# Second reciprocal spread as three bf16 parts, its split on VectorE around the first scales, and selectors built while the first inputs land

## The chip, the cores and the metric

One core of one Trainium2 chip. The metric is the device time of one execution in microseconds (us); most kernels ran several times, and all those runs are of the fast state; three kernels ran only once, which leaves their state unknown, and of these only the profiles are used. A profile is one execution; its span is some 1.8 us shorter than the time that is reported for it (291.8 against 293.62 for the first one).

## The reference

Linear attention with the feature map elu(x) + 1 over 8 batches, 8 heads, 576 tokens and a head width of 64, then a two-layer network with g(h) = h - tanh(h).

```python
def phi(x): return np.where(x > 0, x, np.exp(x) - 1.0) + 1.0
q_p, k_p = (phi(q), phi(k))
kv = np.einsum('bhsd,bhse->bhde', k_p, v)
z = np.sum(k_p, axis=2)
num = np.einsum('bhsd,bhde->bhse', q_p, kv)
den = np.einsum('bhsd,bhd->bhs', q_p, z)[..., None] + 1e-06
# x = (num / den), heads side by side: [4608, 512]
h = x @ w_in                 # [4608, 2048]
out = (h - np.tanh(h)) @ w_out   # [4608, 512]
```

All inputs are fp32 in memory. The loads that GpSimd issues turn them into bf16 on the way.

## The kernel before

The token axis is worked in nine chunks of 512. TensorE writes into banks numbered 0 to 7, and another engine has to empty a bank before it is written again. Before chunk 0 can begin, batch 0 has to pass through attention; this opening fills the first 18 us or so. 1/den lies as one row per token group and head (`rden`), and it must be spread over the 64 channels of each head. TensorE does this with a matmul by a 0/1 selector, a "spread". In batch 0 the spread is fp32, for head pairs 0 and 2 first, for 1 and 3 later:

```python
    def b0_spread(pairs, n0):
        for n, p in enumerate(pairs):
            for t in range(4):
                r = slice(32 * t, 32 * t + 32)
                nc.tensor.matmul(ps_all[:, 4 + t, 128 * (n0 + n):128 * (n0 + n) + 128],
                                 sel[r, p].rearrange("p h e -> p (h e)"), rden_t[0][r, 0:128], start=True, stop=True)
    ...
    load_q(0)
    load_k(0)
    make_identity(nc, ident)      # GpSimd, as the loads
    load_v(0)
    ...                           # w_in in ten pieces
    load_k(1); load_wo(0); load_wo(1); load_q(1)
    ...                           # GpSimd memsets
    load_v(1); load_wo(2); load_wo(3)
    ...
    b0_spread((0, 2), 0)
    b0_scale(0, ns0, 0, 0, 4)
    b0_scale(0, ns0, 0, 4, 8)
    b0_scale(2, ns0, 1)
    b0_num(1, ns0)                # TensorE into banks 2 and 3, then a ScalarE copy out of them

    def open2():
        b0_spread((1, 3), 2)
        b0_scale(1, ns0, 2)
        b0_scale(3, ns0, 3)
    ...
    # chunk 0, hidden blocks 0 to 3 in banks 0 to 3, as (head pair, block)
            order = [((0, 0), (0, 1)), ((2, 0), (2, 1), (0, 2), (0, 3), (2, 2), (2, 3)),
                     [(p, fi) for p in (1, 3) for fi in range(4)]]
            for n, part_ in enumerate(order):
                if n == 1:
                    open2()
                ...
```

In the second layer of chunk 0 TensorE goes through four groups of four steps, one quarter of `w_out` for each group. Batch 1's attention lies between these steps: its q is transposed and its k and v are multiplied just ahead of the third group. In batch 1 the spread is already done from three bf16 parts that lie in three bands of the rows, so that one matmul adds them up (`a_split`, with the selector `sel3`); `prepare` builds that selector on VectorE in the second layer of chunk 0.

Of the kernel before, what the change touches and what calls it, by code (L numbers as in the profile page):

```python
# [18 lines left out]
def kernel(  # L19
# [80 lines left out]
    def load_q(b):  # L100
        q_t[b] = kpool.tile([128, 2, 2, J, D], BF16, name="qraw")
        load(b, q_t[b], q, b == 0)
# [124 lines left out]
    def b0_num(i, ns):  # L227
# [4 lines left out]
                             qT[:, i, 0:8, hg, :], start=True, stop=True)  # L232
        nc.scalar.copy(ns[:, i::2, 0:8, :].rearrange("p a j t -> p a (j t)"), ps_all[:, b0:b0 + 2, :])

    def b0_spread(pairs, n0):

        for n, p in enumerate(pairs):
# [4 lines that stand above are left out]
# [164 lines left out]
    act0 = rpool.tile([128, 1], F32, name="act0")  # L406
    nc.scalar.activation(act0, zero[:, 0:1], AF.Exp)
    load_q(0)
    load_k(0)
    make_identity(nc, ident)  # L410
    load_v(0)
    for f0, n in ((0, 256), (256, 256), (512, 512), (1024, 512), (1536, 512)):
        load_wi(f0, n)
# [22 lines left out]
    for n in range(3):  # L436
        e0 = float(np.float32(rest).astype(ml_dtypes.bfloat16))
        nc.vector.memset(eps[32 * n:32 * n + 1], e0)
        rest -= e0


    def spin(n):
        for _ in range(n):
# [2 lines left out]
    side = Banks([4, 5, 6, 7])  # L446
    kz_t[0] = kz_c[0]
    (eq0, rq0, mq0), (eq1, rq1, mq1) = (phi_pieces(0, q_t, qp_t, "qp", i) for i in range(2))
    for f in (eq0, rq0, mq0, eq1, rq1, mq1):
        f()  # L450
    spin(18)
# [3 lines left out]
        f()  # L455
    spin(5)
    a_qT_pe(0, 1, side, "AA")

    for t in range(4):
        nc.scalar.copy(s8[32 * t:32 * t + 32, 0].rearrange("q h p -> q (h p)"),  # L460
                       ident[32 * t:32 * t + 32, 32 * t:32 * t + 8])
    nc.scalar.copy(sel, s8[:, 0].rearrange("q h p -> q p h").unsqueeze(3).to_broadcast([128, NP, 2, 64]))
    spin(6)
    b0_z(0)
# [10 lines left out]
    b0_num(0, ns0)  # L475
    b0_kv(1)
    b0_kz(1)
    b0_spread((0, 2), 0)

    b0_scale(0, ns0, 0, 0, 4)  # L480
    b0_scale(0, ns0, 0, 4, 8)
    b0_scale(2, ns0, 1)
    b0_num(1, ns0)

    def open2():
        b0_spread((1, 3), 2)
        b0_scale(1, ns0, 2)
        b0_scale(3, ns0, 3)

    def prepare():  # L490

        for t in range(4):
            nc.vector.tensor_copy(s8[32 * t:32 * t + 32, 1:3].rearrange("q n h p -> q (n h p)"),
                                  ident[32 * t:32 * t + 32, 32 * t + 8:32 * t + 24])
        s24 = rpool.tile([128, 2 * NP], F32, name="s24")
        f8 = s8.rearrange("q n h p -> q n (h p)")
        nc.vector.tensor_add(s24, f8[:, 1], f8[:, 2])
        nc.vector.tensor_reduce(part[:, 0:1], s24, mybir.AxisListType.X, ALU.add, negate=True)
        nc.vector.tensor_reduce(part[:, 1:2], f8[:, 2], mybir.AxisListType.X, ALU.add, negate=True)
        nc.vector.tensor_add(s24, s24, f8[:, 0])  # L500
        nc.vector.tensor_copy(
            sel3, s24.rearrange("q (h p) -> q p h", h=2).unsqueeze(3).to_broadcast([128, NP, 2, 64]))

    for c in range(NC):
        gT = gpool.tile([128, NF, 512], BF16, name="gT")
        n1, n2 = c + 1, c + 2
        s1 = {i: [] for i in range(16)}
        s2 = {i: [] for i in range(16)}
        if c == 0:
            side = Banks([4, 5, 6, 7])  # L510
            sub = {}

            def spread1(h):
                sub["bp"] = a_spread_pe(1, 4, (2 * h, 2 * h + 1))
                for p in (2 * h, 2 * h + 1):
                    a_scale(1, p, sub["ns"], sub["bp"], 144 * (p % 2))

            def num1():
                sub["ns"] = new_ns(1)
                for p in (NP, 0, 1, 2, 3):  # L520
                    a_num_copy(1, sub["ns"], p, side)

            s1[11].append(lambda: a_kphi(1, 0))
            s1[13].append(lambda: a_kphi(1, 1))
            s2[3].append(lambda: a_qphi(1, 0))
            s2[4].append(lambda: (a_qphi(1, 1), load_q(2), load_k(2), load_v(2)))
            s2[0].append(prepare)
            s2[7].append(lambda: (a_qT_pe(1, 0, side), a_kv(1, side), a_qT_pe(1, 1, side)))
            s2[8].append(lambda: b0_scale_rest(side))
            s2[9].append(lambda: (a_den(1, side), num1(), a_split(1)))  # L530
            s2[11].append(lambda: spread1(0))

            qs, ks = [], []

            def exp2(pieces, src, store, name, i):
                pieces.append(phi_pieces(2, src, store, name, i))
                pieces[i][0]()

            def rest2(f):
                f[1]()  # L540
                f[2]()

            s2[11].append(lambda: (exp2(qs, q_t, qp_t, "qp", 0), rest2(qs[0])))
            s2[12].append(lambda: exp2(qs, q_t, qp_t, "qp", 1))
            s2[13].append(lambda: (spread1(1), exp2(ks, k_t, kp_t, "kp", 0), rest2(qs[1]), a_qT_dma(2)))
            s2[14].append(lambda: rest2(ks[0]))
        elif n1 < B:
            s1[8 if c == 1 else 5].append(lambda: a_kv_cols(n1, attn))
            s1[10 if c == 1 else 8].append(lambda: (a_den(n1, attn), a_spread(n1)))
            for p in range(NP + 1):  # L550
                s2[(11 if c == 1 else 9) + p].append(lambda p=p: a_num(n1, p))
        if c == 1:
            s1[1].append(lambda: a_kphi(2, 1))
            s1[3].append(lambda: (a_vp(2, 0), a_vp(2, 1)))
        if c >= 1 and n2 < B:

            s1[0].append(lambda: (gate(qT_t[n1]), load_k(n2), load_q(n2), load_v(n2)))
            d = 2
            s2[d].append(lambda: a_kphi(n2, 0))
            s2[d + 2].append(lambda: a_kphi(n2, 1))  # L560
            s2[d + 4].append(lambda: a_qphi(n2, 0))
            s2[d + 6].append(lambda: (a_qphi(n2, 1), a_qT_dma(n2)))
            for i in range(2):
                s2[14 + i].append(lambda i=i: a_vp(n2, i))
        if c == 0:

            first = Banks([4, 5, 6, 7, 0, 1, 2, 3])
            hs = [ps_all[:, n, :] for n in range(4)]
            order = [((0, 0), (0, 1)), ((2, 0), (2, 1), (0, 2), (0, 3), (2, 2), (2, 3)),
                     [(p, fi) for p in (1, 3) for fi in range(4)]]  # L570
            seen = [0] * 4
            for n, part_ in enumerate(order):
                if n == 1:
                    open2()
                for x in range(2 if n == 0 else 0):
                    for p, fi in part_:
                        nc.tensor.matmul(hs[fi][:, 256 * x:256 * x + 256], w_in_sb[:, 0, fi * 128:(fi + 1) * 128],
                                         xT[:, p, 256 * x:256 * x + 256], start=(x == 0), stop=False)
                        seen[fi] = 1
                for p, fi in part_ if n else ():  # L580
                    l1mm(c, fi, hs[fi], p, seen[fi])
                    seen[fi] += 1
            for fi in range(4):
                l1act(fi, hs[fi], gT)
        for fi in range(4 if c == 0 else 0, NF):
            h = first() if c == 0 else dense()
            for p in range(NP):
                l1mm(c, fi, h, p, p)
            if c == 0:
                l1act(fi, h, gT)  # L590
            elif fi % 2:
                n = dense.order[(dense.n - 1) % 6]
                l1act2(fi - 1, ps_all[:, n - 1:n + 1, :], gT)
            for f in s1[fi]:
                f()
        os_ = {}
        for s in range(16):

            (g, i) = divmod(s, 4) if c == 0 else (s % 4, s // 4)
            if g == 0:  # L600
                os_[i] = ps_all[:, i, :] if c == 0 else dense()
            if c == NC - 1 and i == 3:

                if g == 0:
                    o2 = dense()
                    for o, f in ((os_[i], slice(0, 384)), (o2, slice(384, DM))):
                        for fi in range(NF):
                            nc.tensor.matmul(o[:, f], gT[:, fi, 384:512], w_out_sb[:, fi, f],
                                             start=(fi == 0), stop=(fi == NF - 1))
                        evac(c, i, o, f.start, f.stop)  # L610
                continue
            l2mm(gT, os_[i], i, 4 * g, 4 * g + 4)
            if g == 3:
                evac(c, i, os_[i])
            for f in s2[s]:
                f()
# [30 lines left out]
```

## Time and profile before

| | before |
|---|---|
| time, median of the first 3 runs | 294.0 us (293.95 to 294.2) |
| span of the profile | 291.8 us |
| TensorE busy | 284.2 us, 97% |
| first spread starts | 14.79 us |
| second layer of chunk 0 starts | 31.10 us |
| third quarter of `w_out` lands | 40.89 us |

A page has one row for each engine over 40 equal slices. The views used here are the timeline (start, duration, engine, line, operation, output and inputs, count, and in brackets the idle time before it with what ended it), the chain that ended last (start, duration, what), and the table of windows (window, length, then the busy time of PE, PEld, DVE, ACT and POOL, granted clock, share of the transfer engines, GB/s). PE is TensorE, PEld its weight loads, DVE VectorE, ACT ScalarE, POOL GpSimd. Line numbers differ between kernels.

### The profile page before, as it was taken

What the parts mean: (1) busy time and instruction counts of PE and PEld (TensorE: products, weight loads), DVE (VectorE), ACT (ScalarE), POOL (GpSimd) and SP (SyncE); (2) the same over time, 40 slices, a digit from 0 to 9 for tenths busy, and PEclk for the clock granted to TensorE, in tenths of its full rate; (3) what the DMA queues carried; (4) which work ended last, traced back from release to release, by engine and by line L of the source; (5) the groups of instructions that cost most, each with busy time, mean ns of one, the idle gap of its engine ahead of it and who ended that gap; (6) DMA issues with size and microseconds to landing.
All of it is one profiled execution on the core that took longest, in us unless ns stands there. A gap on an engine that the chain in (4) does not pass through costs nothing.

```text
span 291.8 us, 4476 instructions
## 1 busy us (share of the span) xinstructions
PE 284.2 (97%) x1775; PEld 134.5 (46%) x1803; DVE 174.8 (60%) x266; ACT 139.7 (48%) x168; POOL 33.1 (11%) x55
## 2 busy tenths in 40 slices
PE   8999999999999999999999999999999999999994
PEld 3544464454454444544444445444444444444443
DVE  4759958987458674776478637865581457106600
ACT  4838638846254733465345534751551155126411
POOL 8673030110030003000300030000000000000000
PEclk9999999999999999999999999999999999999999
DMA  6999999998989668955795579766117310130032
GB/s 96 198 204 212 208 207 213 214 168 145 253 158 159 170 131 135 200 139 127 134 223 131 120 137 196 144 142 139 32 34 168 73 36 0 42 84 20 0 74 72
DMA packets 39077, 38.94 MB, mean 133 GB/s; under 512 B 16336, under 2 KB 33808, under 8 KB 38288
## 3 DMA queue, kind: packets, MB, share of 16 engines
q0 software_dynamic: 17552, 18.35, 39.0%
q1 hardware_dynamic: 21344, 20.17, 30.5%
q8 instruction: 14, 0.23, 0.3%
q10 hardware_dynamic: 160, 0.13, 0.1%
q14 instruction: 7, 0.06, 0.1%
HBM read 43.91 MB, written 9.55 MB: 183 GB/s over the span
## 4 chain that ended last, share of the span: by engine, by line
PE 75%; DMA 18%; POOL 2%; issue 1%; SPq 1%; DVE 1%; ACT 1%; DVEq 0%; POOLq 0%
PE ps_all L366 37%; PE ps_all L387 32%; DMA w_out_sb<-in_moe_w_out_dram 6%; DMA w_in_sb<-in_moe_w_in_dram 3%; DMA rdb<-ds 3%; DMA out_dram<-osb 2%; PE ps_all L199 2%; DMA kraw<-in_k_dram 2%; PE ps_all L317 2%; DMA ds<-rden 1%; PE ps_all L276 1%; POOL v L419 1%; ACT osb L396 1%; SPq L401 0%; POOL qraw L90 0%
## 5 line engine op out<-in xcount | busy, mean ns | idle before, releaser
L366 PE MATMUL ps_all<-xT,w_in_sb 128*128 128x512 bf16 x558 | 126.5, 380 | 0.9 <-issue 0.2
L387 PE MATMUL ps_all<-w_out_sb,gT 128*128 128x512 bf16 x548 | 126.2, 380 | 0.7
L373 DVE TENSOR_TENSOR gT<-ps_all,th 128x1024 bf16<-128x1024 f32 x64 | 77.9, 1218 | 59.7 <-ACT th L372 59.7
L372 ACT ACTIVATE th<-ps_all 128x1024 f32<-128x1024 f32 x64 | 65.5, 1023 | 57.0 <-PE ps_all L366 46.4
L366 PEld LDWEIGHTS <-w_in_sb 128*128 128x128 bf16 x574 | 55.0, 98 | 66.0
L387 PEld LDWEIGHTS <-gT 128*128 128x128 bf16 x560 | 54.1, 98 | 64.7 <-issue 0.6
L396 ACT COPY osb<-ps_all 128x512 f32<-128x512 f32 (+1 forms) x36 | 20.8, 582 | 72.3 <-PE ps_all L387 55.9
L328 DVE TENSOR_TENSOR xT<-ps_all,rdb 128x512 bf16<-128x512 f32 x24 | 16.3, 689 | 13.7 <-PE ps_all L317 11.2
L134 ACT ACTIVATE e<-qraw 128x1152 bf16<-128x1152 bf16 x16 | 18.5, 1161 | 7.3 <-DMA qraw<-in_q_dram 7.3
L134 ACT ACTIVATE e<-kraw 128x1152 bf16<-128x1152 bf16 x15 | 17.4, 1162 | 0.1
L136 DVE TENSOR_TENSOR qp<-e,r 128x1152 bf16<-128x1152 bf16 x16 | 12.1, 758 | 7.8 <-ACT e L134 7.0
L136 DVE TENSOR_TENSOR kp<-e,r 128x1152 bf16<-128x1152 bf16 x15 | 11.4, 758 | 7.9 <-ACT e L134 7.0
L383 POOL COPY g<-qT 1x1 bf16<-1x1 bf16 x5 | 0.9, 182 | 119.7 <-DMA qT<-qp 119.7
L378 DVE TENSOR_TENSOR gT<-ps_all,th 128x512 bf16<-128x512 f32 x16 | 10.3, 686 | 2.3 <-ACT th L377 1.7
L377 ACT ACTIVATE th<-ps_all 128x512 f32<-128x512 f32 x16 | 9.2, 598 | 4.4 <-PE ps_all L366 3.2
L444 PE MATMUL ps_all<-zero 128*128 128x512 bf16 x29 | 9.3, 487 | 1.2 <-DVE zero L405 1.2
L317 PE MATMUL ps_all<-qT,kz 128*128 128x512 bf16 x28 | 10.1, 380 | 0.1
L135 DVE TENSOR_SCALAR r<-qraw 128x1152 bf16<-128x1152 bf16 x16 | 7.3, 453 | 1.9 <-DMA qraw<-in_q_dram 1.9
L199 PEld LDWEIGHTS <-kp 64*128 64x128 bf16 x216 | 6.4, 94 | 2.5 <-issue 2.5
L285 DVE RECIPROCAL rden<-den 128x144 f32<-128x144 f32 x7 | 7.4, 1052 | 0.2
L199 PE MATMUL ps_all<-vp,kp 64*128 64x136 bf16 x216 | 7.4, 220 | 0.0
L394 DVE COPY osb<-ps_all 128x128 f32<-128x128 f32 x1 | 0.3, 291 | 11.6 <-DMA out_dram<-osb 11.6
(84 smaller groups left out, 123.0 us busy)
## 6 DMA issues: line engine op xcount, KB each, us to landing
out_dram<-osb SPq DMA_DIRECT2D x70, 128.0 KB
rdb<-ds SPq DMA_DIRECT2D x12, 576.0 KB
kraw<-in_k_dram POOLq DMA_DIRECT2D x7, 576.0 KB, 7.1
qraw<-in_q_dram POOLq DMA_DIRECT2D x7, 576.0 KB, 9.2
v<-in_v_dram POOLq DMA_DIRECT2D x7, 576.0 KB, 11.9
w_out_sb<-in_moe_w_out_dram POOLq DMA_DIRECT2D x4, 512.0 KB, 16.0
w_in_sb<-in_moe_w_in_dram POOLq DMA_DIRECT2D x6, 256.0 KB, 8.6
qraw<-in_q_dram POOLq DMA_DIRECT2D x2, 288.0 KB, 4.4
```

What stands on the lines that cost most here:

```text
L134: return (lambda: nc.scalar.activation(e, x, AF.Exp), lambda: nc.vector.tensor_scalar(r, x, 0.0, 1.0, ALU.max, ALU.add), lambda: nc.vector ...
L136: lambda: nc.vector.tensor_tensor(y, e, r, ALU.min))
L199: nc.tensor.matmul(ps[hg][:, i, :], kp[r, i, j].rearrange("p h d -> p (h d)"), vp[r, i, j, :], start=(j == 0), stop=(j == J - 1))
L317: nc.tensor.matmul(ps, kz[:, p // 2, p % 2, 0:128], qT[:, p % 2, 0:8, p // 2, :], start=True, stop=True)
L328: nc.vector.tensor_mul(xT[:, p, S * b:S * b + 512].rearrange("p (j t c) -> p j t c", j=8, t=4), ps.rearrange("p j (t c) -> p j t c", t=4), ...
L366: nc.tensor.matmul(h, w_in_sb[:, 2 * (p % 2) + p // 2, fi * 128:(fi + 1) * 128], xT[:, p, c * 512:(c + 1) * 512], start=(n == 0), stop=(n ...
L372: nc.scalar.activation(th, h, AF.Tanh)
L373: nc.vector.tensor_sub(gT[:, fi:fi + 2, :], h, th)
L378: nc.vector.tensor_sub(gT[:, fi, :], h, th)
L387: nc.tensor.matmul(o, gT[:, fi, i * 128:(i + 1) * 128], w_out_sb[:, fi, :], start=(fi == 0), stop=(fi == NF - 1))
L396: nc.scalar.copy(osb[:, f0:f1], o[:, f0:f1])
L444: nc.tensor.matmul(ps_all[:, 0, :], zero[:, 0:128], zero, start=True, stop=True)
```

## The change

The intent is to shorten TensorE's work in the opening. The second spread takes three bf16 parts instead of fp32. The parts are made on VectorE, the first half of the work ahead of the first scales, in a hole, and the second half behind them. Since their selector is now needed at the start, `prepare` moves there, and the identity that it reads goes ahead of k on GpSimd. On TensorE three dense matmuls go ahead of the second spread, to cover the wait for the parts.

```diff
+    def b0_split():
+        f = rden_t[0][:, 0:128]
+        t1, t2, w = (rpool.tile([128, J * 16], BF16, name=n)[:, 0:128] for n in ("t1", "t2", "w"))
+        u = rpool.tile([128, J * 16], F32, name="u")[:, 0:128]
+        nc.vector.tensor_copy(t1, f)
+        nc.vector.scalar_tensor_tensor(u, t1, part[:, 0:1], f, ALU.mult, ALU.add)
+        yield
+        nc.vector.tensor_copy(t2, u)
+        nc.vector.scalar_tensor_tensor(w, t2, part[:, 1:2], u, ALU.mult, ALU.add)
+        rden_t[0] = w
+        yield
+    def b0_spread3(pairs, n0):        # as b0_spread, with sel3 and w
 ...
     load_q(0)
+    make_identity(nc, ident)
     load_k(0)
-    make_identity(nc, ident)
 ...
+    prepare()                         # ahead of the first work on q; its code is moved here
-    for t in range(4):
-        nc.scalar.copy(s8[32 * t:32 * t + 32, 0]...,  ident[...])
 ...
+    split0 = b0_split()
+    next(split0)
     b0_spread((0, 2), 0)
     b0_scale(0, ns0, 0, 0, 4)
     b0_scale(0, ns0, 0, 4, 8)
     b0_scale(2, ns0, 1)
+    next(split0)
     b0_num(1, ns0)
     def open2():
-        b0_spread((1, 3), 2)
+        b0_spread3((1, 3), 2)
 ...
-            s2[0].append(prepare)
 ...
-            order = [((0, 0), (0, 1)), ((2, 0), (2, 1), (0, 2), (0, 3), (2, 2), (2, 3)),
+            order = [((0, 0), (0, 1)), ((0, 2), (0, 3), (2, 0)), ((2, 1), (2, 2), (2, 3)),
                      [(p, fi) for p in (1, 3) for fi in range(4)]]
-                if n == 1:
+                if n == 2:
                     open2()
```

More of the change, by code (lines that the diff above doesn't have):

```diff
@@ L233, in b0_num @@
         nc.scalar.copy(ns[:, i::2, 0:8, :].rearrange("p a j t -> p a (j t)"), ps_all[:, b0:b0 + 2, :])
+    def b0_split():
[10 more added lines that the diff above has]
+    def b0_spread3(pairs, n0):
+        for n, p in enumerate(pairs):
+            for t in range(4):
+                r = slice(32 * t, 32 * t + 32)
+                nc.tensor.matmul(ps_all[:, 4 + t, 128 * (n0 + n):128 * (n0 + n) + 128],
+                                 sel3[r, p].rearrange("p h e -> p (h e)"), rden_t[0][r], start=True, stop=True)
     def b0_spread(pairs, n0):
@@ L439, with prepare @@
         rest -= e0
+    def prepare():
+        for t in range(4):
+            nc.vector.tensor_copy(s8[32 * t:32 * t + 32].rearrange("q n h p -> q (n h p)"),
+                                  ident[32 * t:32 * t + 32, 32 * t:32 * t + 24])
+        s24 = rpool.tile([128, 2 * NP], F32, name="s24")
+        f8 = s8.rearrange("q n h p -> q n (h p)")
+        nc.vector.tensor_add(s24, f8[:, 1], f8[:, 2])
+        nc.vector.tensor_reduce(part[:, 0:1], s24, mybir.AxisListType.X, ALU.add, negate=True)
+        nc.vector.tensor_reduce(part[:, 1:2], f8[:, 2], mybir.AxisListType.X, ALU.add, negate=True)
+        nc.vector.tensor_add(s24, s24, f8[:, 0])
+        nc.vector.tensor_copy(
+            sel3, s24.rearrange("q (h p) -> q p h", h=2).unsqueeze(3).to_broadcast([128, NP, 2, 64]))
     def spin(n):
@@ L457 @@
     a_qT_pe(0, 1, side, "AA")
-    for t in range(4):
-        nc.scalar.copy(s8[32 * t:32 * t + 32, 0].rearrange("q h p -> q (h p)"),
-                       ident[32 * t:32 * t + 32, 32 * t:32 * t + 8])
     nc.scalar.copy(sel, s8[:, 0].rearrange("q h p -> q p h").unsqueeze(3).to_broadcast([128, NP, 2, 64]))
@@ L482 @@
     b0_scale(2, ns0, 1)
+    next(split0)
     b0_num(1, ns0)
     def open2():
-        b0_spread((1, 3), 2)
+        b0_spread3((1, 3), 2)
         b0_scale(1, ns0, 2)
         b0_scale(3, ns0, 3)
-    def prepare():
-        for t in range(4):
-            nc.vector.tensor_copy(s8[32 * t:32 * t + 32, 1:3].rearrange("q n h p -> q (n h p)"),
-                                  ident[32 * t:32 * t + 32, 32 * t + 8:32 * t + 24])
-        s24 = rpool.tile([128, 2 * NP], F32, name="s24")
-        f8 = s8.rearrange("q n h p -> q n (h p)")
-        nc.vector.tensor_add(s24, f8[:, 1], f8[:, 2])
-        nc.vector.tensor_reduce(part[:, 0:1], s24, mybir.AxisListType.X, ALU.add, negate=True)
-        nc.vector.tensor_reduce(part[:, 1:2], f8[:, 2], mybir.AxisListType.X, ALU.add, negate=True)
-        nc.vector.tensor_add(s24, s24, f8[:, 0])
-        nc.vector.tensor_copy(
-            sel3, s24.rearrange("q (h p) -> q p h", h=2).unsqueeze(3).to_broadcast([128, NP, 2, 64]))
     for c in range(NC):
```

## The prediction

> **What bounds the kernel now.** I read the page from the top: busy shares, the slices, then the chain that ended last. The page of the kernel before:
>
> ```profile
> PE 284.2 (97%) x1775; PEld 134.5 (46%) x1803; DVE 174.8 (60%) x266; ACT 139.7 (48%) x168; POOL 33.1 (11%) x55
> PE   8999999999999999999999999999999999999994
> DMA  6999999998989668955795579766117310130032
> PE 75%; DMA 18%; POOL 2%; issue 1%; SPq 1%; DVE 1%; ACT 1%; DVEq 0%; POOLq 0%
> ```
>
> TensorE is busy for 97% of the span, so one first thinks that any TensorE time saved is time saved. But the fourth line says that 18% of the chain is transfers, and the DMA row stays at 8 or 9 far past the first 40 us (5.5 slices of 7.3 us). So I asked for the chain in order of time, up to 60 us:
>
> ```profile
> 9.24 8.93 DMA w_in_sb<-in_moe_w_in_dram
> ...
> 23.05 17.84 DMA w_out_sb<-in_moe_w_out_dram
> 40.89 0.04 issue
> 40.93 0.38 PE ps_all L387
> ```
>
> Up to 40.89 us the chain runs through transfers, the last of them the third quarter of the output weights; only then does TensorE take over and keep it to the end. The timeline of TensorE around that point:
>
> ```profile
> 38.60 1.66 PE L177 MATMUL ps_all<-v,kp 64*128 64x192 bf16 x36
> 40.20 0.68 PE L164 MATMUL ps_all<-ident,qp 128*128 128x128 bf16 x9
> 40.93 1.02 PE L387 MATMUL ps_all<-w_out_sb,gT 128*128 128x512 bf16 x3
> ```
>
> The nine transposes begin some 0.06 us apart (the first such group began at 38.01, the work behind it at 38.60: 0.59 for nine), so the matmul behind the second group could have begun at 40.20 + 0.59 = 40.79. Its weights were loaded at 40.65. It began at 40.93, 0.04 us after the landing. TensorE thus waits there for about 0.14 us, though no wait is printed, because the matmul spans overlap. The change works between 3 and 20 us, all before this point. A gain there is kept only so far as that quarter lands earlier.
>
> Do the transfers have slack? Table of windows (us, the busy time of PE, PEld, DVE, ACT, POOL, then clock, DMA share, GB/s):
>
> ```profile
> 14.00:26.00 12.00, 11.45 (x95) 5.91 (x96) 8.40 (x15) 6.85 (x12) 8.72 (x13) 1.00 1.27 209
> 26.00:40.00 14.00, 13.95 (x99) 7.28 (x100) 11.89 (x27) 9.30 (x13) 1.64 (x3) 1.00 1.22 206
> ```
>
> 206 to 209 GB/s without a break, counted as bf16 written; the source is fp32, so twice that, some 412 to 418 GB/s, is read. The transfer queue is full and nothing in the change takes bytes out of it.
>
> **What the Trainium skill says.** "DMA: Bandwidth & Descriptors", Bandwidth, has 425 GB/s measured for a 16 MB load and a fabric ceiling of 435. The trace's 412 to 418 read, if I count the fp32 side, agrees: the loads run at their rate. "SBUF — State Buffer", section "SBUF: two separate sides", says that a VectorE operation in a 2-port mode, such as an fp32 copy within SBUF, locks GpSimd out of writing the descriptors of its own DMAs. This bears on the change, because the selectors are now built while GpSimd issues k and v. The trace before shows no such stall there, since VectorE is idle from 3.5 to 5.42. "FP8 and Floating Point Precision" gives true fp32 four passes through the array. The trace decides: the 16 fp32 calls in the two spreads show as 32 matmuls, so two records for a call, of 271 ns and with weight loads of 186 ns; the bf16 spread of batch 1 shows one record for a call, 226 ns, with loads of 92 ns.
>
> **The change, part by part.**
>
> 1. The second spread. Eight fp32 calls become eight bf16 ones. The rows of the timeline for the two kinds:
>
> ```profile
> 17.05 0.73 PE L240 MATMUL ps_all<-rden,sel 32*128 32x128 f32 x16 [0.22 <-DVE xT L244]
> 17.93 13.33 PE L366 MATMUL ps_all<-xT,w_in_sb 128*128 128x512 bf16 x60 [0.16 <-issue]
> 46.16 0.30 PE L354 MATMUL ps_all<-w,sel 32*128 32x144 bf16 x8
> ```
>
> 0.73 becomes about 0.30: 0.43 us less on TensorE.
>
> 2. The split on VectorE. In batch 1 its four operations take 238, 367, 236 and 369 ns, 1.21 us, with starts so spaced that the four fill 44.78 to 46.11. For 128 instead of 144 columns I take 0.62 us for each half. VectorE before:
>
> ```profile
> 14.72 0.42 DVE L225 TENSOR_TENSOR kz<-ps_all,mask 128x256 bf16<-128x256 f32 x1
> 15.64 1.35 DVE L244 TENSOR_TENSOR xT<-ns,ps_all 128x256 bf16<-128x256 f32 x3 [0.50 <-PE ps_all L240]
> 17.91 1.28 DVE L244 TENSOR_TENSOR xT<-ns,ps_all 128x512 bf16<-128x512 f32 x2 [0.92 <-PE ps_all L240]
> ```
>
> The first half goes into the hole from 15.14 to 15.64: it ends at 15.16 + 0.62 = 15.78, so the three scales begin 0.15 late, at 15.80, and end at 17.15. The second half ends at 17.15 + 0.03 + 0.62 = 17.80. The spread can't begin before.
>
> 3. The order on TensorE. Three dense matmuls now come ahead of the spread. Two of them write banks 2 and 3, which ScalarE empties until 16.09 + 1.01 = 17.10. So they start at 17.15, and with 0.22 each (13.33 less the 0.38 of the last, over 59) the three end at 17.8. The spread runs from about 18.0 to 18.3. Its two scales run from 18.4 to 19.7, three more dense matmuls fill 18.25 to 18.9, and the four of head pair 1 wait for the first scale, to 19.1. With eight left, this opening ends at 19.1 + 8 x 0.22 = 20.85. Before, it ended at 17.93 + 14 x 0.22 = 21.0. TensorE gains about 0.15 us (0 to 0.5 if I have placed a wait wrongly), not the 0.43.
>
> 4. The selectors. The block of building moves from 34.06 to 35.81 us to about 3.5, and takes the same 1.75 us; it ends near 5.25, before q lands at 5.42. At its old place VectorE had room (the q of batch 1 only lands at 35.5), so nothing is gained there. ScalarE loses four casts, 0.81 us, from 12.68. But the first spread waits for the reciprocal, which ends at 14.64, and not for the selector that ScalarE finished at 14.14. Nothing is gained.
>
> 5. The identity ahead of k. GpSimd needs 0.62 us for it (4.20 to 4.82), so the issue of k goes from 2.78 to 3.4. The packets of q fill the engines until about 6.3, and q needed 4.2 us from issue to landing, with 1.4 us of that its own data at 205 GB/s. So k's descriptors are due at 3.4 + 2.8 = 6.2: just in time, a close thing.
>
> **Sum.** TensorE comes to the third quarter of the weights 0.15 us earlier and waits 0.29 instead of 0.14. The chain keeps its transfers until 40.89. Net 0.0, at most 0.1: 294.0 becomes 293.9.
>
> **Rivals.** (a) Transfers don't bound, since the wait of 0.14 rests on 0.06 us spacings: then all of the TensorE gain arrives, 0.15 to 0.5 us, 293.5 to 293.85. For it, the 97% busy; against it, the start 0.04 us after the landing. (b) k's later issue leaves a hole in the transfers, helped by VectorE's lock: all later landings, the third quarter too, slip by up to 0.6 us, and so does the end: 294.3 to 294.6. For it: between 6.5 and 7.0 the rate is down to 97 GB/s already. Against it: the DMA share there is still 0.89, so the engines had packets then, only slow ones. (c) VectorE becomes the bound of the opening: each half of the split delays a scale, and if the second spread is later than I think, TensorE loses up to 0.3 us at 20 us. It has 0.14 us of waiting at 40.79 to hide that in, so 294.0 to 294.2.
>
> **Range and chances.** The three runs before span 0.25 us. From 0.5 us of gain in (a) to 0.6 us of loss in (b), 293.4 to 294.6 should hold it 8 times in 10. 2% is 5.9 us. Nothing that the change touches is that large: the whole of TensorE's waiting before 41 us is under 4 us. So same has 0.98.
>
> **What would show it.** In the changed kernel's profile, the second spread has 8 bf16 records near 18.0 in about 0.30 us; the first three scales begin near 15.8; the dense stream reaches 20.85 instead of 21.0; the selectors are built from 3.5 to 5.3; k lands at 8.95 as before; the chain still turns from the output weights to TensorE at 40.9, and TensorE waits there 0.3 us instead of 0.14. Wrong would be: a landing of that quarter moved by over 0.3 us either way, or a k that lands late.

## The result, and the profile after

| | before | after |
|---|---|---|
| time, median of 5 runs | 294.1 us (293.95 to 294.2) | 294.03 us (293.73 to 294.73) |
| ratio, 95% interval | | 1.0003 (0.9989 to 1.0018) |
| span of the profile, granted clock | 291.8 us, 1.000 | 292.6 us, 0.998 |

A ratio is the mean time of one kernel's runs over the mean of the other's runs of the same rounds, so it isn't quite the ratio of the medians in the table. The two kernels are the same in time.

The chain in order of time, kernel after, at the point where transfers hand over to TensorE:

```profile
9.31 9.88 DMA w_in_sb<-in_moe_w_in_dram
...
23.82 17.72 DMA w_out_sb<-in_moe_w_out_dram
41.54 0.04 issue
41.58 1.02 PE ps_all L408 x4
```

The form is that of before: up to the landing of the third quarter of the output weights the chain is transfers and, in the lines cut here, GpSimd's work between them (19.18 to 23.82 us), and TensorE starts 0.04 us after the landing. The landing is 0.65 us later than in the first profile of before. That needed looking into (runs `before_again` and `after_again`).

TensorE's timeline in the opening and up to the third group, kernel after:

```profile
16.19 0.71 PE L598 MATMUL ps_all<-xT,w_in_sb 128*128 128x256 bf16 x4
17.23 0.81 PE L387 MATMUL ps_all<-xT,w_in_sb 128*128 128x512 bf16 x3 [0.33 <-ACT ns L233]
17.97 0.29 PE L253 MATMUL ps_all<-w,sel 32*128 32x128 bf16 x8
18.19 13.18 PE L387 MATMUL ps_all<-xT,w_in_sb 128*128 128x512 bf16 x59
31.21 7.07 PE L408 MATMUL ps_all<-w_out_sb,gT 128*128 128x512 bf16 x32
38.16 0.68 PE L164 MATMUL ps_all<-ident,qp 128*128 128x128 bf16 x9
39.06 1.66 PE L177 MATMUL ps_all<-v,kp 64*128 64x192 bf16 x36 [0.22 <-DMA v<-in_v_dram]
40.65 0.68 PE L164 MATMUL ps_all<-ident,qp 128*128 128x128 bf16 x9
41.58 1.02 PE L408 MATMUL ps_all<-w_out_sb,gT 128*128 128x512 bf16 x4 [0.25 <-DMA w_out_sb<-in_moe_w_out_dram]
```

The bf16 spread is there, with 8 records, and the next matmul starts 0.22 us after it began. But the brackets are new: 0.33 us until ScalarE has emptied banks 2 and 3, and later two waits for transfers that the profile now prints. VectorE and GpSimd beside it, kernel after:

```profile
15.14 0.22 DVE L240 CAST t<-rden 128x128 bf16<-128x128 f32 x1
15.39 0.35 DVE L241 SCALAR_TENSOR_TENSOR u<-t,part,rden 128x128 f32<-128x128 bf16 x1
15.72 1.35 DVE L265 TENSOR_TENSOR xT<-ns,ps_all 128x256 bf16<-128x256 f32 x3
16.70 0.75 POOL L115 DMA_DIRECT2D w_out_sb<-in_moe_w_out_dram  x1
16.98 0.52 DVE L243 CAST t<-u 128x128 bf16<-128x128 f32 x1
17.54 0.35 DVE L244 SCALAR_TENSOR_TENSOR w<-t,part,u 128x128 bf16<-128x128 bf16 x1
18.38 1.29 DVE L265 TENSOR_TENSOR xT<-ns,ps_all 128x512 bf16<-128x512 f32 x2 [0.49 <-PE ps_all L253]
```

The first half of the split fits its hole. In the second half the cast takes 0.52 us where the same cast ahead of the scales took 0.22; GpSimd was issuing a load from 16.70 to 17.45.

Weight-load lines add what the matmul lines hide. In the kernel after, they show a pause that the row of 59 matmuls swallows: the fourth matmul behind the spread starts at 19.12, when the first scale of head pair 1, begun at 18.38 and 0.69 us long, is done (timeline, weight loads):

```profile
18.19 0.55 PEld L387 LDWEIGHTS <-w_in_sb 128*128 128x128 bf16 x4
19.12 11.75 PEld L387 LDWEIGHTS <-w_in_sb 128*128 128x128 bf16 x55 [0.39 <-issue]
```

The same view of the kernel before:

```profile
17.70 13.06 PEld L366 LDWEIGHTS <-w_in_sb 128*128 128x128 bf16 x62
```

There are 62 weight loads here, and 60 matmul records in the row at 17.93 that the prediction shows. Two records are missing from the trace. One is the first of the stream: the loads begin one spacing earlier, at 17.70, so the dense stream of before began near 17.72, not 17.93. The other is in the middle: record by record, one start is at 28.51 and the next at 28.94, twice the spacing of 0.216 that the others have.

### The profile page after: what moved, and what is told of

It is laid out like the page before. It is cut to its first block, busy times and chain, and to the rows that moved or that the text cites. A ratio compares the mean times of both kernels' runs of the same rounds, so it can differ in the third digit from the quotient of the medians.

```text
span 292.6 us, 4488 instructions
## 1 busy us (share of the span) xinstructions
PE 285.1 (97%) x1795; PEld 133.8 (46%) x1795; DVE 176.5 (60%) x270; ACT 139.1 (48%) x164; POOL 33.2 (11%) x55
## 4 chain that ended last, share of the span: by engine, by line
PE 77%; DMA 17%; POOL 2%; DVE 1%; SPq 1%; issue 1%; ACT 0%; DVEq 0%; POOLq 0%
PE ps_all L387 37%; PE ps_all L408 34%; DMA w_out_sb<-in_moe_w_out_dram 6%; DMA w_in_sb<-in_moe_w_in_dram 3%; DMA rdb<-ds 3%; PE ps_all L199 2%; PE ps_all L338 2%; DMA kraw<-in_k_dram 2%; DMA out_dram<-osb 2%; DMA ds<-rden 2%; PE ps_all L297 1%; POOL v L440 1%; POOL qraw L90 0%; ACT osb L417 0%; DVE rden L306 0%
## 5 line engine op out<-in xcount | busy, mean ns | idle before, releaser
L387 PE MATMUL ps_all<-xT,w_in_sb 128*128 128x512 bf16 x574 | 127.8, 379 | 0.4 <-ACT ns L233 0.3
L408 PE MATMUL ps_all<-w_out_sb,gT 128*128 128x512 bf16 x560 | 127.6, 379 | 0.3 <-DMA w_out_sb<-in_moe_w_out_dram 0.3
L480 PE MATMUL ps_all<-zero 128*128 128x512 bf16 x29 | 8.6, 454 | 1.2 <-DVE zero L426 1.2
```

The costliest lines, as they stand in the source:

```text
L387: nc.tensor.matmul(h, w_in_sb[:, 2 * (p % 2) + p // 2, fi * 128:(fi + 1) * 128], xT[:, p, c * 512:(c + 1) * 512], start=(n == 0), stop=(n ...
L408: nc.tensor.matmul(o, gT[:, fi, i * 128:(i + 1) * 128], w_out_sb[:, fi, :], start=(fi == 0), stop=(fi == NF - 1))
```

## The experiments

The runs went in three batches, each on another chip and with its own runs of the kernel before; so a ratio is taken within a batch, and times of different batches aren't compared. The batches are the runs from `before_again` to `after_no_v1`, those from `old_order` to `extra_bytes`, and the rest.

My theory once the result was in had two parts. First, the landing of the third quarter of the output weights sets the end. Second, TensorE gains nothing in the opening to begin with, since new waits have taken the place of the 0.45 us that the spread lost. The rivals: the change does save TensorE 0.15 us (as predicted) or the whole 0.45, and only the transfers hide it; or transfers don't matter.

Two measures are read from each profile. A is the time from the first spread's start to the start of the second layer. It holds the whole opening that changed, and leaves out when the inputs landed. B is the time from the start of the second layer to its third group. It holds the waits for batch 1's v and for the third quarter of the weights.

| profile | first spread | A | B | third quarter lands | span, clock |
|---|---|---|---|---|---|
| before | 14.79 | 16.31 | 9.83 | 40.89 | 291.8, 1.000 |
| before_again | 15.07 | 16.31 | 10.09 | 41.42 | 292.1, 0.999 |
| after | 14.86 | 16.35 | 10.37 | 41.54 | 292.6, 0.998 |
| after_again | 14.66 (a record missing) | 16.34 | 10.28 | 41.24 | 291.9, 1.000 |
| before_no_v1 | 15.01 | 16.31 | 9.61 | no wait | 291.6, 0.997 |
| before_no_v1_b | 14.80 | 16.31 | 9.61 | no wait | 291.8, 1.000 |
| after_no_v1 | 14.92 | 16.35 | 9.75 | no wait | 291.8, 0.999 |
| selectors_only | 14.62 | 16.31 | 10.18 | 41.07 | 292.1, 0.997 |
| old_order | 14.26 | 16.67 | 9.95 | 40.84 | 291.6, 1.000 |
| order_only | 15.13 | 16.79 | 9.61 | no wait | 292.2, 1.000 |
| extra_bytes | 14.47 | 16.35 | 11.56 | 42.34 | 293.2, 0.998 |

### Both kernels once more

The two kernels were run as they are. Expected of before_again:

> The kernel before, unchanged, run as if it were a change: it gives the scatter of the method and a second profile. Theory (the landing of the third quarter of the output weights sets the end): ratio 1.000 within 0.0015, and in the profile the span less that landing is 250.9 us as in the first profile (291.8 less 40.89), wherever the landing falls between 40.5 and 41.7. Rival (the landing in the first profile only happened to fall there): span and landing vary on their own, and span less landing differs by more than 0.3 us.

Measured: 293.83 us, ratio 0.9992 (0.9979 to 1.0006). The landing was 41.42, the span less the landing 250.7.

Expected of after_again:

> The changed kernel, unchanged. Theory: ratio 1.000 within 0.002, and span less the landing of the third quarter 251.0 us (292.6 less 41.54 in its first profile), whatever the landing. If the later landing of the first profile (41.54 against 40.89) was a chance of that run, the second lies nearer to 40.9; if the change causes it (k issued later, GpSimd held up by VectorE), it is again 0.4 or more later than in the kernel before.

Measured: 293.87 us, ratio 0.9993 (0.9980 to 1.0006); landing 41.24, span less landing 250.7. The chain of before_again and then of after_again, at the turn:

```profile
23.62 17.80 DMA w_out_sb<-in_moe_w_out_dram
41.42 0.04 issue
41.47 0.38 PE ps_all L387
```

```profile
23.30 17.94 DMA w_out_sb<-in_moe_w_out_dram
41.24 0.04 issue
41.28 0.38 PE ps_all L408
```

The same kernel before lands its quarter at 40.89 and at 41.42, so 0.5 us of scatter is the transfers' own. The later landing of the first profile after isn't shown to come from the change: with k issued near 3.3 us and no bytes added, the landings of the four profiles (after, after_again, selectors_only, old_order) go from 40.84 to 41.54, around the two of before. Over the seven profiles of kernels whose third group waits for it (the table's first four, and selectors_only, old_order and extra_bytes), span less landing is 250.7 to 251.1 while the landing itself goes from 40.84 to 42.34.

### The transfer taken away: before_no_v1 and after_no_v1

Batch 1's v isn't loaded; its buffer is filled with ones. Their outputs are wrong, which doesn't matter for the times. The same edit in both kernels:

```diff
-    for i in (1, 0):
-        nc.gpsimd.memset(v_b[i][:, 2], 1.0)
+    nc.gpsimd.memset(v_b[1], 1.0)
+    nc.gpsimd.memset(v_b[0][:, 2], 1.0)
-    load_v(1)
     load_wo(2)
```

> Kernel before without the transfer of batch 1's v (its buffer is filled with ones by GpSimd, so batch 1's output is wrong on purpose): 0.59 MB as bf16 taken out ahead of the third quarter of the output weights, which then lands near 38.2. Theory: TensorE no longer waits at the third group of the second layer; its first matmul there starts about 40.8 instead of 40.93, and the span shrinks by 0.1 to 0.2 us: ratio 0.9995. Rival (transfers free, TensorE alone bounds): no change of that start. Against this kernel the next run is to be held.

> Changed kernel without the transfer of batch 1's v, wrong on purpose in the same way. Here no transfer hides what TensorE gains or loses by the change. Theory (new waits for the emptied banks and the first scale have eaten the 0.44 us that the bf16 spread saves): third group of the second layer starts within 0.15 us of the run without that transfer of the kernel before, and the two times agree within 0.1%. Rival (the change does save TensorE 0.15 us as I predicted, or 0.4, and only the transfers hide it): starts 0.15 to 0.45 us earlier, span as much shorter.

Measured: before_no_v1 293.75 us, ratio to the kernel before 0.9991 (0.9978 to 1.0005); after_no_v1 293.37 us, ratio 0.9974 (0.9961 to 0.9986), both with the same runs of before. TensorE's timeline of before_no_v1, then of after_no_v1:

```profile
15.01 0.73 PE L240 MATMUL ps_all<-rden,sel 32*128 32x128 f32 x16
...
31.32 7.07 PE L387 MATMUL ps_all<-w_out_sb,gT 128*128 128x512 bf16 x32
...
40.42 0.68 PE L164 MATMUL ps_all<-ident,qp 128*128 128x128 bf16 x9
40.93 1.03 PE L387 MATMUL ps_all<-w_out_sb,gT 128*128 128x512 bf16 x3
```

```profile
14.92 0.73 PE L261 MATMUL ps_all<-rden,sel 32*128 32x128 f32 x16
...
31.27 6.85 PE L408 MATMUL ps_all<-w_out_sb,gT 128*128 128x512 bf16 x31
...
40.50 0.68 PE L164 MATMUL ps_all<-ident,qp 128*128 128x128 bf16 x9
41.02 1.03 PE L408 MATMUL ps_all<-w_out_sb,gT 128*128 128x512 bf16 x3
```

The start of the third group in before_no_v1 is 40.93, as in the first profile before, and not the 40.8 that was expected: its first spread came 0.22 us later (15.01 against 14.79). So only B, which leaves that out, shows whether a wait is gone. With the transfer gone, the third group follows 0.51 us after the transposes begin, in both. B without a wait is 9.61, and the waits in it were 0.22 us in the first profile before (not the 0.14 that I took), 0.48 in the second, 0.76 and 0.67 in the two of after. In after_no_v1, 0.14 of B is a wait of another kind (0.18 us for batch 1's q work on VectorE is printed).

A is 31.32 - 15.01 = 16.31 in the kernel before and 31.27 - 14.92 = 16.35 in the kernel after. It repeats within 0.01 us over all profiles. The change costs TensorE 0.04 us; it saves none. That much of the theory is shown.

The times didn't quite keep to it. The expectation was agreement within 0.1%; 293.37 against 293.75 is 0.13%, with intervals of plus or minus 0.13% that overlap. A can't make this difference, since it goes the other way. The start of the opening might; see id_only_no_v1 below.

### One part at a time: old_order, order_only, selectors_only

Each of these three kernels ran once, with a profile. Their times (293.36, 293.99 and 293.86 us) say nothing against a scatter of 0.5 us; A, which repeats within 0.01 us, does.

old_order is the changed kernel with TensorE's former order (the spread ahead of the six dense matmuls):

```diff
-            order = [((0, 0), (0, 1)), ((0, 2), (0, 3), (2, 0)), ((2, 1), (2, 2), (2, 3)),
+            order = [((0, 0), (0, 1)), ((2, 0), (2, 1), (0, 2), (0, 3), (2, 2), (2, 3)),
-                if n == 2:
+                if n == 1:
```

> Changed kernel with TensorE's old order (the spread ahead of the six dense matmuls). Measure: from the start of the first spread to the start of the second layer, 16.31 us in three profiles of the old second spread and 16.35 in three of the new. Theory: the bf16 spread can't start before its third part is there, 2.7 to 3.0 us after the first spread began, so the dense stream starts no earlier than the 2.93 of before; 16.35 to 16.65. Rival (the new order alone eats the saving): 15.9, the whole 0.44 saved.

A = 30.93 - 14.26 = 16.67, just above the 16.35 to 16.65 expected. VectorE and TensorE, timeline of old_order:

```profile
16.38 0.50 DVE L243 CAST t<-u 128x128 bf16<-128x128 f32 x1
16.91 0.35 DVE L244 SCALAR_TENSOR_TENSOR w<-t,part,u 128x128 bf16<-128x128 bf16 x1
17.32 0.29 PE L253 MATMUL ps_all<-w,sel 32*128 32x128 bf16 x8 [1.02 <-DVE w L244]
```

Here TensorE stands still for 1.02 us until the third part is there. So the bf16 spread alone is worse than the fp32 one by 0.36 us: what TensorE saves in the spread, it waits for in the split. Of the 0.36, 0.28 is the cast, which here too takes 0.50 instead of 0.22 us beside a load issue of GpSimd (16.07 to 16.82); without that, by my estimate from these two times, the loss would be 0.08.

order_only is the kernel before with the new order and the fp32 spread:

```diff
-            order = [((0, 0), (0, 1)), ((2, 0), (2, 1), (0, 2), (0, 3), (2, 2), (2, 3)),
+            order = [((0, 0), (0, 1)), ((0, 2), (0, 3), (2, 0)), ((2, 1), (2, 2), (2, 3)),
-                if n == 1:
+                if n == 2:
                     open2()
```

> Kernel before with only the new order on TensorE, its second spread still fp32. Theory: the spread starts about 3.1 after the first, takes 0.67 instead of 0.22, and head pair 1 waits as much longer for its scale: 16.75 to 16.8. Rival (the waits in the opening hide the spread's length here): 16.35.

A = 31.92 - 15.13 = 16.79. The order alone costs 0.48 us. The second scales come 0.85 us later (19.10 - 15.13, against 17.91 - 14.79 before), and TensorE has three dense matmuls instead of six to fill the time until the first of them is done. Order and bf16 together give back 0.44 of it (16.79 to 16.35), the whole saving of the spread; so the spread's length does lie on TensorE's path there, and the order has paid for it in advance. Its TensorE comes to the third group so late that the weights are there: B is 9.61, without a wait, in a kernel that loads everything.

selectors_only is the kernel before with the identity ahead of k and `prepare` at the start, and nothing else:

```diff
     load_q(0)
+    make_identity(nc, ident)
     load_k(0)
-    make_identity(nc, ident)
+    prepare()            # ahead of the first work on q
-            s2[0].append(prepare)
```

> Kernel before with only the identity ahead of k and the selectors built at the start; old order, fp32 spread, no split. Theory: nothing on the path: 16.31; the first half of k lands within the 8.95 to 9.3 of the two profiles of before; k's issue starts near 3.35. Rival (the later issue of k or VectorE's lock costs): k lands 0.4 or more later than 9.3, or the first spread starts later than 15.1.

A = 30.93 - 14.62 = 16.31, k's issue at 3.33, the first work on k at 9.03. Nothing is lost by the earlier selectors.

### Bytes added: extra_bytes

The changed kernel with one more load, which nobody reads, ahead of the third quarter of the weights:

```diff
     load_v(1)
+    extra = const.tile([128, 2, J, D], BF16, name="extra")
+    nc.gpsimd.dma_start(out=extra..., in_=v[1]...[0])    # 0.29 MB as bf16
     load_wo(2)
```

> Changed kernel with one more transfer that nobody reads, 0.29 MB as bf16, ahead of the third quarter of the output weights. Theory (that landing sets the end): 0.295 MB at 206 GB/s is 1.43 us, so the landing moves to about 42.8 and the time goes up by as much, to 295.4: ratio 1.005. Rival (transfers hidden, TensorE the bound): ratio 1.000 to 1.001.

Measured: 294.96 us against 293.82 for the kernel before in the same batch, ratio 1.0038 (1.0022 to 1.0055). The changed kernel without the load had 1.0003 and 0.9993. The chain of extra_bytes at the turn:

```profile
23.69 18.64 DMA w_out_sb<-in_moe_w_out_dram
42.34 0.04 issue
42.38 1.02 PE ps_all L408 x4
```

The landing moved by 1.1 us against after_again and by 0.8 against the first profile after, and the time by 1.1. The 1.43 that I had worked out is too much by a quarter or more; since one landing scatters by 0.5, a single profile can't say why. The direction and the fit of time and landing are what the theory said, and the rival (no more than 1.001) is out.

### k's issue and the dip in the rate

Looking through the profiles I saw something that I hadn't asked about: between 6 and 7.5 us the rate of the transfers is low in the kernel before. The table of windows, before and then after:

```profile
6.00:7.50 1.50, 1.50 (x8) 0.61 (x7) 0.89 (x2) 1.30 (x2) 1.50 (x4) 1.00 1.09 138
```

```profile
6.00:7.50 1.50, 1.09 (x6) 0.29 (x3) 0.77 (x2) 1.29 (x2) 1.50 (x4) 1.00 1.20 196
```

Three runs without batch 1's v should tell what does it. id_only_no_v1 has only the identity ahead of k; delay_k_no_v1 puts a memset ahead of k and leaves the identity behind it:

```diff
+    nc.gpsimd.memset(vp[:, 0, 0:4, :].rearrange("p j c -> p (j c)"), 0.0)
     load_k(0)
     make_identity(nc, ident)
```

> Kernel before without batch 1's v transfer (wrong on purpose), with only the identity ahead of k on GpSimd. In the ten profiles so far the rate of the transfers from 6 to 7.5 us is 138 to 174 GB/s with k issued at 2.78 and 196 to 206 with k issued at 3.33, and the first spread starts at 14.8 to 15.1 against 14.3 to 14.9. Theory (the place of the identity does it): 195 or more, first spread at 14.3 to 14.9, and a time 0.2 to 0.4 us under the run without v of the kernel before, as the changed kernel without v has (293.37 against 293.75). Rival (the selectors on VectorE or chance do it): 140 to 175 and no difference in time.

> Kernel before without batch 1's v, with a memset of some 0.55 us on GpSimd ahead of k and the identity left behind k. Tells what it is about the place of the identity. Theory A (k's later issue removes the dip): rate from 6 to 7.5 us 195 or more, first spread 14.3 to 14.9. Theory B (GpSimd's work between k's and v's issue makes the dip): 140 to 175, first spread 14.8 to 15.2.

> Kernel before without batch 1's v once more, as the yardstick on the same chip as the two runs above. Dip of the rate from 6 to 7.5 us to 140 to 175 GB/s, first spread at 14.8 to 15.1, ratio to the kernel before 0.999.

| | rate 6 to 7.5 us | first spread | time | ratio to before, 95% |
|---|---|---|---|---|
| before_no_v1_b | 179 | 14.80 | 293.42 | 0.9988 (0.9976 to 1.0001) |
| id_only_no_v1 | 199 | 15.36 | 293.14 | 0.9978 (0.9964 to 0.9991) |
| delay_k_no_v1 | 204 | 14.63 | 293.55 | 0.9995 (0.9982 to 1.0007) |

In the rate, theory A holds: delaying k's issue removes the dip, whether the identity or a memset delays it. Over all profiles, the five with k issued at 2.8 show 138 to 179 GB/s, the nine with k issued near 3.3 show 195 to 206. Why, no view tells. In the time it isn't settled. id_only_no_v1 had no dip and yet its first spread came latest of all, at 15.36, where 14.3 to 14.9 was expected; but its profile is of the slowest of its five executions (293.74, the others 292.98 to 293.21). And delay_k_no_v1 is no faster than before_no_v1_b. Between 293.14 and 293.55 the intervals overlap. So the 0.13% of after_no_v1 stays open: it may be the earlier opening or scatter.

### A try at a better kernel: halves

If the waits in B are the cost, another order of loads should take them away. This kernel is the one before with the identity ahead of k, batch 1's v in two halves around the third quarter of the weights, the second half of its accumulation two steps later and all behind it one step later:

```diff
-    load_v(1)
+    <first half of v[1]>
     load_wo(2)
+    <second half of v[1]>
     load_wo(3)
-            s2[7].append(lambda: (a_qT_pe(1, 0, side), a_kv(1, side), a_qT_pe(1, 1, side)))
+            s2[7].append(lambda: (a_qT_pe(1, 0, Banks([4, 5])), kv1(0), a_qT_pe(1, 1, Banks([4, 5]))))
+            s2[9].append(lambda: (kv1(1), kz1()))
-            s2[9].append(lambda: (a_den(1, side), num1(), a_split(1)))
-            s2[11].append(lambda: spread1(0))
+            s2[10].append(lambda: (a_den(1, Banks([5])), num1(), a_split(1)))
+            s2[12].append(lambda: spread1(0))
...
```

> A try at a better kernel, right results: kernel before with the identity ahead of k, and batch 1's v loaded in two halves with the third quarter of the output weights between them; the second half of that batch's accumulation moves two steps later in the second layer and what follows it one step later. Theory: the waits of 0.2 to 0.45 us at the third group fall away, ratio 0.998 to 0.9995. Rival (the later scales hold up the first layer of chunk 1): a wait of 0.3 us or more near 50 us, ratio 1.000 or above.

Measured: 294.85 us against 293.8, ratio 1.0034 (1.0022 to 1.0047), correct. The waits of B did fall: the third group starts at 40.32, 0.56 us after the transposes before it. The rival came true all the same. TensorE's timeline of halves in chunk 1:

```profile
50.64 7.44 PE L366 MATMUL ps_all<-xT,w_in_sb 128*128 128x512 bf16 x32
58.55 1.02 PE L366 MATMUL ps_all<-xT,w_in_sb 128*128 128x512 bf16 x4 [0.48 <-DVE gT L373]
```

and VectorE's, which explains the wait:

```profile
53.68 0.45 DVE L135 TENSOR_SCALAR r<-kraw 128x1152 bf16<-128x1152 bf16 x1
54.24 0.76 DVE L136 TENSOR_TENSOR kp<-e,r 128x1152 bf16<-128x1152 bf16 x1
54.92 1.22 DVE L373 TENSOR_TENSOR gT<-ps_all,th 128x1024 bf16<-128x1024 f32 x1
```

The work on batch 2, shifted behind the later scales, keeps VectorE busy until the first subtraction of chunk 1 (`gT`) begins at 54.92, though ScalarE had its tanh ready at 53.69; banks come free late, and TensorE waits 0.48 us at 58.55. The kernel before prints no wait of TensorE from 45 to 70 us. The printed wait is only half of it: from the start of chunk 1's first layer to the k and v matmuls inside it, halves takes 8.87 us (50.64 to 59.51) and the kernel before 7.86 (50.20 to 58.06), which is 1.0 us more, as much as the loss in time. No version that beats both kernels came of this.

## Why the prediction was right or wrong, point by point

- **What bounds.** Right. The landing of the third quarter of the output weights sets the end: span less landing stays within 250.7 to 251.1, a load added ahead of it costs 1.1 us, and with a load less B loses its wait. The size was off: TensorE's wait there was 0.22 us, not 0.14, because nine transposes take 0.51 and not 0.59 from start to start.
- **Part 1, the spread.** Right: 0.22 us from start to start of the next, against 0.67.
- **Part 2, the split.** Right for the first half (scales at 15.72, predicted 15.80). In the first profile the second half ended at 17.89 instead of 17.80, but by another way: the cast was held up beside GpSimd's load issue. In after_again the cast took 0.22 us and the third part was ready at 17.38, and the spread still started at 17.76, behind the dense matmuls that waited for the banks. So in the new order the split isn't what the spread waits for.
- **Part 3, the order, "TensorE gains about 0.15 us".** Wrong, the mis-sized step of the sum. The opening after is as predicted (three matmuls at 17.23, spread at 17.97, the wait for the first scale). What failed is the figure for before. The "17.93" from which I took it was the start of the first recorded matmul, and the record before it is missing; the spacing of 0.22 came from the same row, stretched by the second missing record. The stream began near 17.72, so that opening ended at 17.72 + 14 x 0.216 = 20.74 and not 21.0 (0.216 is 31.10 - 17.72, over 62). The gain is -0.04 us: the 0.45 saved in the spread came back as 0.11 more until the banks are there (17.23 - 16.19, against 17.05 - 16.12), 0.09 between the third dense matmul and the spread, and 0.27 for the first scale at 19.12.
- **Parts 4 and 5, selectors and identity.** Right that neither lies on the path: selectors_only leaves A at 16.31, and k isn't later. The block took longer than the 1.75 us predicted, 3.51 to 5.73, since its last cast takes 0.71 us there against 0.43 at its old place; VectorE therefore takes up q at 5.65, up to 0.22 us after ScalarE (5.43 in old_order). That costs nothing, for the product behind both waits for ScalarE. GpSimd's two issues of v took 0.73 and 0.78 us beside it, against 0.72 each before: the lock that the prediction names cost no more than that. "Just in time, a close thing" was too wary: the rate between q and k rose instead.
- **The sum.** 293.9 was predicted, 294.03 measured, for a reason half right: there was hardly a TensorE gain for the transfers to hide.
- **The rivals.** (a) is out by A. (b) is out by selectors_only and by the landings, which overlap. (c), VectorE as the bound, is in part what happened: in old_order TensorE waits 1.02 us for the split, and the new order turns that into waits for banks and scales.
- **What would have shown it wrong.** I named a landing moved by over 0.3 us. It did move, by 0.65. The test was too tight, for the kernel before moves its own landing by 0.53 between two profiles.

## What to carry to other kernels

A share of 97% on one engine doesn't say that this engine sets the end: follow the chain in order of time to the last point where something else hands over, and ask of each saving whether it lies before that point. When an operation is made shorter by giving its inputs more work elsewhere, measure from a fixed event before it to a fixed event after it; here 0.45 us saved in the spread came back as waits for banks and for the first scale, to within 0.04. Before you take the first matmul's time from a timeline, hold its count against the count of the weight loads.

## What the Trainium skill lacked or had wrong

- "SBUF — State Buffer", section "Who interferes with whom", says that of a VectorE operation in a 2-port mode and GpSimd whoever issues first gets the shared ports, and that the other fully blocks. It has no figure for VectorE blocked by a load's issue, and the runs show a limit: VectorE's cast that starts 0.28 to 0.31 us after GpSimd's load issue (after, old_order, extra_bytes) takes 0.50 to 0.52 us and ends 0.05 us after that issue ends; started 0.22 us after it (after_again, after_no_v1) it takes 0.22, so it isn't blocked for the whole issue of 0.75 us. That the shared ports are the cause is not shown here.
- "DMA: Bandwidth & Descriptors", section "Where 436 GB/s comes from", says without a condition that for transfers between HBM and SBUF the HBM side, about 358 GB/s, binds. Here a program on one core shows 206 to 209 GB/s written as bf16 from 14 to 40 us; counted on the fp32 side, by my estimate, some 412 to 418 read. That is above the 358 and near the 425 that the page's table has for a large load; the note under that table says that its figures are for one core alone and that about 358 is left with both cores of the pair streaming.
- No page has the dip: 138 to 179 GB/s from 6 to 7.5 us when the next load's issue came at 2.8 us, 195 to 206 when at 3.3.
- "FP8 and Floating Point Precision" counts four passes for true fp32. The trace shows two records for a call, and eight calls of 128 columns on 32 rows take 0.67 us against 0.22 us in bf16, a factor of three.
